# Attention thresholds made on the scalar engine instead of the vector engine

## The chip, the cores and the metric

The kernel runs on one core of a Trainium2 chip. Its time is device microseconds (us) of one execution, start to end. Five engines work at once, each through its own queue in order: TensorE (PE, matrix products; its weight loads are listed as PEld), VectorE (DVE), ScalarE (ACT), GpSimd (POOL) and SyncE (SP, which here issues DMA transfers). They wait for each other on semaphores.

## What is computed

Attention over 4 batches, 8 heads, 576 positions, 64 dimensions, in which only scores close to the row's maximum count; its output goes through a mixture of experts with a greedy assignment of tokens, and through a gated feed-forward layer. The change is in the attention alone, whose reference is:

```python
scores = scale * np.matmul(q, k.transpose(0, 1, 3, 2))
thresh = np.max(scores, axis=-1, keepdims=True) - tau
scores = np.where(scores >= thresh, scores, -1000000000.0)
scores = scores - np.max(scores, axis=-1, keepdims=True)
attn = np.exp(scores)
attn = attn / (np.sum(attn, axis=-1, keepdims=True) + 1e-09)
return np.matmul(attn, v).astype(np.float32)
```

## The kernel before

The attention is cut into 16 units; a unit is one head of two batches and has nine score tiles of 128 rows by 576 columns. A score tile goes through these steps:

- PE makes the scores in PSUM, `s` (L248).
- DVE takes the negated maximum of each row, `nm` (L259), one column of a buffer of two columns that two successive tiles share.
- ACT makes `e` = exp(s + nm) (L263).
- For every second tile DVE makes the thresholds `th` of both tiles of the pair at once, a 128x2 result (L267): minus `nm`, minus the non-negative part of tau (`taup`, made once).
- DVE masks: `p` = e where s >= th, else 0, with the row sum on the way (L281). Both masks of a pair need `th`; the mask of the even tile comes first.
- PE transposes `p` (L289). The transposed blocks `t` are split into two parts, `hi` and `lo`, on ACT (L319, L322, L327, L344), DVE (L346, L349) and POOL (L185, L335); PE multiplies with the values (L361, L365, L373), ACT copies out `ot` (L378), PE multiplies again (L389, L394), and ACT scales by `ri`, one over the row sum (L416), which DVE makes (L401, L402).

POOL meanwhile prepares the next units' inputs (L198, L202, L212, L220 and again L185). DVE also converts pieces of the later layers' weights in three steps (L583, L585, L587), and at the end of a group of eight heads it sums the router's logits (L436, L439, L441).

The order of the work on every engine is written out beforehand. Each step has a name and a time in a table, `TAB` (the last two units: `LAST`), for two units together, a period of 2 x 18.2795 us; all steps are sorted by time, and each engine gets its own in that order. The times in the table decide the order alone; at run time an engine waits only for its semaphores. The two score buffers are freed by the masks, so PE's next scores wait for them. Four pairs of `nm` and `th` are kept.

After the attention (about the first 355 us) come the routing of tokens and the experts' products, in an order that a planner makes from costs of its own.

Of the kernel before, what the change touches and what calls it, by code (L numbers as in the profile page):

```python
# [7 lines left out]
F32 = mybir.dt.float32  # L8
# [3 lines left out]
AF = mybir.ActivationFunctionType  # L12
OP = mybir.AluOpType
# [112 lines left out]
def attention(tc, raw, prep, qk, v, tau, wg, xd, lg, idf, filler, chosen):  # L126
    nc = tc.nc
    with (
# [10 lines left out]
        taur = cp.tile([128, 1], F32, name="taur")  # L139
# [2 lines left out]
        warm = cp.tile([128, 1], F32, name="warm")  # L142
        nid = cp.tile([128, 128], F32R, name="nid")
        c = cp.tile([128, 1], F32, name="c")
        taup = cp.tile([128, 1], F32, name="taup")

        def constants():
            nc.vector.memset(warm, 0.0)
            nc.scalar.activation(warm, warm, AF.Exp)
            nc.vector.tensor_scalar(nid, idf, -1.0, None, op0=OP.mult)  # L150
            for o in (0, 64):
                nc.vector.tensor_copy(r2[o : o + 64, :, 0:64], idf[o : o + 64, o : o + 64].unsqueeze(1).to_broadcast([64, 8, 64]))
            nc.vector.tensor_scalar(c, taur, 0.0, 0.125, op0=OP.is_ge, op1=OP.mult)
            nc.vector.tensor_scalar(taup, taur, 0.0, None, op0=OP.max)

        def load_wg():
            for o in (0, 64):
# [3 lines left out]
        ev = []  # L161
# [2 lines left out]
            ev.append((t, len(ev), fn, args))  # L164

        def on(u, name, fn, *args):
            ev.append((2 * P * (u // 2) + (LAST if u >= 14 else TAB)[name], len(ev), fn, args))

        def types(u):
            return (LAST_TYPES if u >= 14 else TYPES)[u % 2]  # L170
# [93 lines left out]

        def sthr(n):
            nm, th = nmth[n // 2]
            nc.vector.tensor_scalar(th, nm, -1.0, taup, op0=OP.mult, op1=OP.subtract)  # L267

        def smask(u, i, n):
            w = d[u]  # L270
# [172 lines left out]
        P = PERIOD  # L443
        V, A, G = nc.vector, nc.scalar, nc.gpsimd
        for u in range(16):
            t = P * u
            pu = u % 2
            at(-100 + u if u < 2 else t - 2 * P, "", load, u)
            if u == 0:
                for n, (lo, hi) in enumerate(((0, 128), (128, 512), (512, 896), (896, 1280))):  # L450
                    steps = split_q(u, lo, hi, A, V)
                    if n < 2:
                        at(-20 + 2 * n, "", run, steps)
                    else:
                        at(TAB["exp1"] + 0.01 * n, "", next, steps)
                        at(TAB["mask1"] + 0.01 * n, "", next, steps)
                for n, (lo, hi) in enumerate(((0, 288), (288, S), (S, KW))):
                    at(-20.5 + 0.5 * n if n < 2 else -17, "", run, split_k(u, lo, hi, A, V if n < 2 else G))
                at(-15, "", run, split_v(u, G))
            else:  # L460
                steps = split(u)
                for n in range(12):
                    on(u, f"pp{pu}.{n}", next, steps)
            for i in range(9):
                n = 9 * u + i
                on(u, f"mm{n%18}", scores, u, i)
                on(u, f"max{n%18}", smax, u, i, n)
                on(u, f"exp{n%18}", sexp, u, i)
                if n % 2:
                    on(u, f"thr{n%18}", sthr, n)  # L470
                on(u, f"mask{n%18}", smask, u, i, n)
            for i in range(11):
# [13 lines left out]
                if i in (4, 10):  # L486
# [3 lines left out]
                    on(u, f"xl{pu}.{w}", l_out, u, w)  # L490
        at(-60, "", load_wg)
        at(-101, "", constants)
        at(14 * P + 40.4, "", chosen, slice(0, 9))
        at(14 * P + LAST["xl1.0"] + 0.01, "", chosen, slice(9, 13))
# [1025 lines left out]
def program(tc, qk, v, tau, wg, w12, cst, csti, w3, out):  # L1520
    nc = tc.nc
    with tc.tile_pool(name="keep", bufs=1) as kp, tc.tile_pool(name="keep_dram", bufs=1, space=bass.MemoryType.DRAM) as dp:
        idf = kp.tile([128, 128], F32, name="idf")
        make_identity(nc, idf)
        lg = kp.tile([128, 18, 8], F32, name="lg")
        xd = dp.tile([2304, 512], F32, name="xd")
        wf = [dp.tile([128, 512], F32, name=f"wf{n}") for n in range(36)]
        words = w3.bitcast(I32)
        rt = Router(tc, lg, idf, kp, dp)
        pre = n_pieces()  # L1530
        with (
            tc.tile_pool(name="at_raw", bufs=2) as rp, tc.tile_pool(name="at_prep", bufs=2) as pp,
            tc.tile_pool(name="staging", bufs=2) as sp,
        ):
            weights = Narrow(
                nc, lambda s: sp.tile([128, 1024], I32, name="wd", bufs=4), lambda n: sp.tile([128, 512], F32, name="wn", bufs=3),
                words, nc.sync, lambda n, f: nc.sync.dma_start(wf[n], f), {n: n % 4 for n in range(pre)},
            )
            filler = fill(rt.prepare(cst, csti), weights, 4)
            attention(tc, rp, pp, qk, v, tau, wg, xd, lg, idf, filler, rt.begin)  # L1540
        experts(tc, rt, xd, idf, w12, words, wf, pre, out)
# [14 lines left out]
```

## Time and profile before

| | |
|---|---|
| Median of 3 runs | 1146.61 us (1145.21 to 1149.75) |
| Profiled execution | 1150.95 us, of which the span of the profile is 1149.2 us |
| Busy over the span | PE 93%, DVE 71%, ACT 45%, POOL 28% |

The span holds very different stages, so the shares of the whole tell little of the attention. In the profile's rows, an entry gives the start and length in us, the engine, the line of the kernel, the operation, out<-in with shapes, a count where equal neighbours are merged, and in brackets the idle time before it with what ended it. A row of stretches gives, for each engine, its busy time in the stretch.

### The profile page before, as it was taken

What the parts mean: (1) busy time and instruction counts of PE and PEld (TensorE: products, weight loads), DVE (VectorE), ACT (ScalarE), POOL (GpSimd) and SP (SyncE); (2) the same over time, 40 slices, a digit from 0 to 9 for tenths busy, and PEclk for the clock granted to TensorE, in tenths of its full rate; (3) what the DMA queues carried; (4) which work ended last, traced back from release to release, by engine and by line L of the source; (5) the groups of instructions that cost most, each with busy time, mean ns of one, the idle gap of its engine ahead of it and who ended that gap; (6) DMA issues with size and microseconds to landing.
All of it is one profiled execution on the core that took longest, in us unless ns stands there. A gap on an engine that the chain in (4) does not pass through costs nothing.

```text
span 1149.2 us, 21045 instructions
## 1 busy us (share of the span) xinstructions
PE 1068.4 (93%) x7884; PEld 990.7 (86%) x7885; DVE 819.8 (71%) x1987; ACT 517.6 (45%) x1104; POOL 323.9 (28%) x334
## 2 busy tenths in 40 slices
PE   4899999999997399999899999999999999999997
PEld 3787878787886268899899999999999899999996
DVE  7999999899998799886776975974974412512411
ACT  4788887688784224333214314313413412412411
POOL 5788887788861101000101010110100100100101
PEclk9999999899998599999899999999999999999999
DMA  7422422422303766537436446546444433533232
GB/s 275 147 85 82 157 84 84 155 85 81 102 1 108 265 222 222 201 130 192 130 98 193 147 132 156 164 119 168 150 129 135 148 111 111 167 111 117 74 113 88
DMA packets 52886, 156.18 MB, mean 136 GB/s; under 512 B 11568, under 2 KB 16560, under 8 KB 50864
## 3 DMA queue, kind: packets, MB, share of 16 engines
q1 hardware_dynamic: 49712, 145.40, 39.5%
q0 software_dynamic: 3072, 9.44, 2.7%
q8 instruction: 62, 1.02, 0.4%
q14 instruction: 40, 0.33, 0.1%
HBM read 135.38 MB, written 19.43 MB: 135 GB/s over the span
## 4 chain that ended last, share of the span: by engine, by line
PE 40%; issue 26%; DVE 25%; DMA 4%; ACT 2%; POOL 2%; SPq 0%; DVEq 0%; POOLq 0%; ACTq 0%
PE ps L1144 18%; PE acc L1154 11%; DVE nm L259 6%; DVE p L281 6%; PE s L248 4%; DVE th L267 3%; DVE lo L346 2%; PE t L289 2%; DMA wr<-in_w 1%; PE o L365 1%; DMA wf<-wf 1%; PE o L373 1%; DVE wf L1088 1%; POOL out L1386 1%; DMA wd<-in_w 1%
## 5 line engine op out<-in xcount | busy, mean ns | idle before, releaser
L1330 DVE TENSOR_TENSOR gt<-ps,sg 128x288 f32<-128x288 f32 x96 | 43.9, 457 | 164.5 <-PE ps L1144 132.9
L1386 POOL DMA_INDIRECT out<-orow,idx x24 | 24.8, 1032 | 408.4 <-ACT orow L1382 404.0
L1326 ACT ACTIVATE sg<-ps 128x288 f32<-128x288 f32 x96 | 39.5, 412 | 193.8 <-PE ps L1144 169.2
L1154 PE MATMUL acc<-gh,wo 128*128 128x288 f32 x768 | 124.6, 300 | 0.9 <-DVE wo L1052 0.9
L263 ACT ACTIVATE e<-s,nm 128x576 f32<-128x576 f32 x144 | 104.9, 741 | 37.6 <-DVE nm L259 35.3
L1052 DVE TENSOR_TENSOR w<-wr,w 128x512 fp32r<-128x512 f32 x112 | 75.6, 689 | 54.7 <-ACT w L1225 53.8
L1144 PE MATMUL ps<-yh,wgh 128*128 128x288 f32 x384 | 107.2, 301 | 6.8 <-ACT orow L1382 4.4
L248 PE MATMUL s<-kh,qs 128*128 128x288 f32 x320 | 80.3, 333 | 34.5 <-DVE p L281 23.6
L1334 ACT ACTIVATE gh<-gt 128x288 fp32r<-128x288 f32 x96 | 42.7, 444 | 149.9 <-DVE gt L1330 149.9
L1154 PEld LDWEIGHTS acc<-gh,wo 128*128 128x128 f32 x768 | 108.3, 189 | 1.2 <-DVE wo L1052 1.1
L259 DVE TENSOR_REDUCE nm<-s 128x1 f32<-128x576 f32 x144 | 104.1, 747 | 5.3 <-PE s L248 4.5
L1144 PE MATMUL ps<-yh,wvh 128*128 128x288 f32 x384 | 107.3, 301 | 0.0
L1169 POOL DMA_INDIRECT xr<-xd,idx x16 | 15.2, 951 | 323.8 <-issue 158.0
L1144 PE MATMUL ps<-yh,wvl 128*128 128x288 f32 x384 | 106.1, 298 | 0.0
L1144 PE MATMUL ps<-yh,wgl 128*128 128x288 f32 x384 | 105.8, 297 | 0.0
L1225 ACT ACTIVATE w<-wr 128x512 fp32r<-128x512 f32 x112 | 69.2, 629 | 75.8 <-PE acc L1154 31.9
L281 DVE SCALAR_TENSOR_TENSOR p<-s,th,e 128x576 f32<-128x576 f32 x128 | 100.1, 808 | 4.3 <-ACT tf L319 0.5
L248 PEld LDWEIGHTS s<-kh,qs 128*128 128x128 f32 x320 | 52.7, 198 | 55.5 <-issue 36.3
L289 PE MATMUL t<-idf,p 128*128 128x128 f32 x548 | 81.5, 282 | 0.9 <-ACT lo L344 0.7
L1144 PEld LDWEIGHTS ps<-yh,wgh 128*128 128x128 f32 x384 | 72.8, 189 | 8.7 <-ACT orow L1382 4.9
L763 DVE TENSOR_SCALAR_CACHE_REDUCE big<-kw,tw 128x1152 bf16<-128x1152 f32 x56 | 78.9, 1409 | 1.0
L289 PEld LDWEIGHTS t<-idf,p 128*128 128x128 f32 x548 | 66.0, 145 | 14.0 <-ACT tf L319 2.2
(233 smaller groups left out, 2794.8 us busy)
## 6 DMA issues: line engine op xcount, KB each, us to landing
wo<-wod SPq DMA_DIRECT2D x84, 512.0 KB, 3.6
wr<-in_w SPq DMA_DIRECT2D x64, 512.0 KB, 3.8
qkr<-in_qk SPq DMA_DIRECT2D x15, 1248.0 KB, 5.7
wd<-in_w SPq DMA_DIRECT2D x36, 512.0 KB, 5.1
wod<-wo SPq DMA_DIRECT2D x12, 512.0 KB, 3.3
vr<-in_v SPq DMA_DIRECT2D x16, 320.0 KB, 3.8
kw<-kx SPq DMA_DIRECT2D x64, 72.0 KB, 4.2
xd<-xl SPq DMA_DIRECT2D x8, 512.0 KB, 4.0
```

Of the source, the lines that this page charges most:

```text
L248: nc.tensor.matmul(s[:, h, 0:288], qs[:, qo : qo + 128], kt[:, ko + 288 * h : ko + 288 * h + 288], start=m == 0, stop=m == len(src) - 1,)
L259: nc.vector.tensor_reduce(d[u]["nm", i], d[u]["s", i][:, :, 0:288], op=OP.max, axis=AX.XY, negate=True)
L263: nc.scalar.activation(e, d[u]["s", i][:, :, 0:288], AF.Exp, bias=d[u]["nm", i])
L281: nc.vector.scalar_tensor_tensor(dst.rearrange("p (c n) -> p c n", c=2), w["s", i][:, :, 0:288], nmth[n // 2][1][:, n % 2 : n % 2 + 1], w[ ...
L289: nc.tensor.matmul(t[:m, 128 * j : 128 * j + 128], src, idf, is_transpose=True, start=j == 0, stop=j == len(srcs) - 1, skip_group_check=True,)
L763: v.tensor_scalar(self.big, self.kw[h], thr, None, op0=OP.is_ge, op1=OP.add, accum_out=cnt[:, h : h + 1])
L1052: V.tensor_sub(l, x, h.bitcast(F32))
L1144: nc.tensor.matmul(ps, w(q), x[:, q], start=n == 0, stop=n == 11)
L1154: nc.tensor.matmul(acc[m][:, :CAP], w[:, 128 * m : 128 * m + 128], x, start=first and i == 0, stop=last and i == 2)
L1225: A.activation(box[nm][:, 0], box["r"][:, i], AF.Copy)
L1330: V.tensor_tensor(box["gt"], box["v"][:, :CAP], box["sg"], op=OP.mult)
L1334: A.activation(box["h"][0], box["gt"], AF.Copy)
```

## The change

The thresholds are made by ACT: `th` = Identity(-1 x nm + ntau), where `ntau` is the negated non-negative part of tau. In the order of the work the step stands where it stood, or directly ahead of the odd tile's exponential (0.01 before it in the table) where that came earlier.

```diff
@@ -142,7 +142,7 @@
-        taup = cp.tile([128, 1], F32, name="taup")
+        ntau = cp.tile([128, 1], F32, name="ntau")
@@ -151,7 +151,7 @@
-            nc.vector.tensor_scalar(taup, taur, 0.0, None, op0=OP.max)
+            nc.vector.tensor_scalar(ntau, taur, 0.0, -1.0, op0=OP.max, op1=OP.mult)
@@ -164,7 +164,9 @@
         def on(u, name, fn, *args):
-            ev.append((2 * P * (u // 2) + (LAST if u >= 14 else TAB)[name], len(ev), fn, args))
+            tab = LAST if u >= 14 else TAB
+            t = min(tab[name], tab["exp" + name[3:]] - 0.01) if name[:3] == "thr" else tab[name]
+            ev.append((2 * P * (u // 2) + t, len(ev), fn, args))
@@ -264,7 +266,7 @@
         def sthr(n):
             nm, th = nmth[n // 2]
-            nc.vector.tensor_scalar(th, nm, -1.0, taup, op0=OP.mult, op1=OP.subtract)
+            nc.scalar.activation(th, nm, AF.Identity, bias=ntau, scale=-1.0)
```

## Rows read from the trace of the kernel before

**Rows 1.** The chain of work that ended last, 0 to 400 us, by line.

```profile
by line: DVE nm L259 16.5%; DVE p L281 16.4%; PE s L248 12.3%; DVE th L267 7.3%; DVE lo L346 5.6%; issue 4.9%; PE t L289 4.9%; PE o L365 3.4%; DMA wf<-wf 3.1%; PE o L373 3.0%; DVE pt L281 1.7%; PE o L361 1.6%; DVE hl L349 1.4%; PE o L389 1.
```

**Rows 2.** Busy time by stretch (two units; two at a group's end): PE, PEld, DVE, ACT, POOL, granted clock, DMA.

```profile
99.24:140.76 41.52, 39.74 (x277) 33.53 (x276) 40.70 (x86) 34.30 (x73) 35.14 (x34) 1.00 0.39 125
...
182.22:230.20 47.98, 43.54 (x277) 37.37 (x276) 42.59 (x89) 34.53 (x73) 35.24 (x34) 0.89 0.33 109
```

**Rows 3.** Line L267 as a group: whole kernel, one stretch of two units, shortest/median/longest.

```profile
L267 DVE TENSOR_SCALAR th<-nm,taup 128x2 f32<-128x2 f32 x72 | 47.1, 654 | 1.2
...
L267 DVE TENSOR_SCALAR th<-nm,taup 128x2 f32<-128x2 f32 x9 | 6.3, 699 | 0.1
...
L267 DVE TENSOR_SCALAR th<-nm,taup x72: 220/572/1548, 9.3 to 347.4; 128x2 f32<-128x2 f32 x72
```

**Rows 4.** DVE in order of time, the stretch from 99 to 142 us.

```profile
100.70 0.53 DVE L267 TENSOR_SCALAR th<-nm,taup 128x2 f32<-128x2 f32 x1
101.14 0.41 DVE L583 TENSOR_SCALAR wn<-wd 128x512 int32<-128x512 int32 x1
...
104.99 0.95 DVE L267 TENSOR_SCALAR th<-nm,taup 128x2 f32<-128x2 f32 x1
105.86 0.16 DVE L401 TENSOR_SCALAR ri<-sm 128x9 f32<-128x9 f32 x1
...
110.73 0.98 DVE L267 TENSOR_SCALAR th<-nm,taup 128x2 f32<-128x2 f32 x1
...
119.87 0.88 DVE L267 TENSOR_SCALAR th<-nm,taup 128x2 f32<-128x2 f32 x1
120.66 0.68 DVE L587 SCALAR_TENSOR_TENSOR wn<-wd,wn 128x512 int32<-128x512 int32 x1
...
124.78 0.23 DVE L267 TENSOR_SCALAR th<-nm,taup 128x2 f32<-128x2 f32 x1
125.11 0.82 DVE L281 SCALAR_TENSOR_TENSOR p<-s,th,e 128x576 f32<-128x576 f32 x1
...
128.64 1.16 DVE L267 TENSOR_SCALAR th<-nm,taup 128x2 f32<-128x2 f32 x1
```

**Rows 5.** POOL in order of time, the same stretch.

```profile
104.37 1.55 POOL L202 TENSOR_TENSOR qs<-qkr,qs 64x640 fp32r<-64x640 f32 x1
...
122.90 1.56 POOL L202 TENSOR_TENSOR qs<-qkr,qs 64x640 fp32r<-64x640 f32 x1
...
128.29 1.48 POOL L212 TENSOR_TENSOR kl<-qkr,kh 128x608 fp32r<-128x608 f32 x1
```

**Rows 6.** DVE and POOL around 198 us.

```profile
197.83 1.00 DVE L585 SCALAR_TENSOR_TENSOR wn<-wd,wn 128x512 int32<-128x512 int32 x1
...
197.56 0.72 POOL L185 TENSOR_SCALAR vh<-vr 128x640 fp32r<-128x640 f32 x1
```

**Rows 7.** ACT's table load, its smallest instruction, and 128x64 ones, as groups.

```profile
L416 ACT ACTIVATE xl<-o,ri 128x64 f32<-128x64 f32 x139 | 31.8, 329 | 0.6 <-PE o L389 0.6
...
L149 ACT ACT_TABLE_LOAD x1 | 1.3, 1283 | 0.7 <-PEq L1549 0.7
...
L149 ACT ACTIVATE warm<-warm 128x1 f32<-128x1 f32 x1 | 0.2, 203 | 0.0
```

**Rows 8.** ACT in order of time, around the odd tiles' exponentials.

```profile
119.27 1.40 ACT L263 ACTIVATE e<-s,nm 128x576 f32<-128x576 f32 x2 [0.52 <-DVE nm L259]
...
133.47 0.59 ACT L319 ACTIVATE tf<-t 128x512 f32<-128x512 f32 x1
...
138.16 0.38 ACT L378 ACTIVATE ot<-o 128x256 f32<-128x256 f32 x1 [0.33 <-PE o L373]
```

**Rows 9.** DVE and PE at 201 to 204 us, and the stretch 206 to 208 us.

```profile
201.22 1.55 DVE L267 TENSOR_SCALAR th<-nm,taup 128x2 f32<-128x2 f32 x1
...
203.85 0.50 PE L248 MATMUL s<-kh,qs 128*128 128x288 f32 x2 [1.88 <-DVE pt L281]
...
206.00:208.00 2.00, 2.00 (x16) 1.87 (x15) 1.97 (x4) 1.47 (x3) 1.84 (x2) 0.50 0.00 1
```

## The prediction

> **What bounds the kernel now.** I read first the chain of work that ended last, for the first 400 us, since the change touches nothing behind the attention. Half of it is DVE: row maxima, masks, splits, and 7.3% on the threshold line itself, which is 29 us of 400 [rows 1]. The reader is to see that a 128x2 instruction stands there beside 128x576 ones.
>
> Second, the busy times by stretch. Two units take 41.5 us, in which DVE is busy for 40.7; it idles 0.8. But PE is busy for 39.7, POOL for 35.1 and ACT for 34.3 [rows 2]. So DVE paces the attention, and PE is only 1.8 us behind it. That is the second thing to see: whatever DVE gives up beyond about 1.8 us in a stretch meets PE, unless part of PE's modelled busy time is itself waiting.
>
> Third, the threshold line as a group: 72 instructions, 47.1 us, mean 654 ns, but from 220 to 1548 ns for one and the same shape [rows 3]. Idle time ahead of them is 1.2 us in all. So the time is spent inside the instruction, and it is not work.
>
> Fourth, therefore, DVE and POOL side by side in order of time. The threshold that starts at 104.99 and takes 0.95 ends at 105.94; the POOL instruction that was running ends at 104.37 + 1.55 = 105.92. The one at 128.64 ends at 129.80, POOL's at 129.77. The one at 124.78 takes 0.23, and POOL's instruction had ended at 124.46 [rows 4, 5]. So this instruction waits for whatever POOL is running. The Trainium skill's page "SBUF — State Buffer", section "Who interferes with whom", states a cause: a tensor_scalar can take a port pair that DVE shares with GpSimd, which is held for a whole instruction, while ACT waits for nobody. The end times above agree with it.
>
> **The change part by part.** The constant `ntau` in place of `taup` is one instruction at the start either way: nothing.
>
> *Taken from DVE.* In a stretch of two units the nine thresholds take 6.3 us. At 0.22 each without a wait that is 2.0 of work and 4.3 of waiting; over the kernel 72 x 0.22 = 15.8 and 31.3 [rows 3]. That is the upper end: 47.1 us, if nothing takes their place.
>
> *What the waits pass on to.* After three of the nine, DVE's next instruction is one that may wait for POOL too: L583 at 101.14, `ri` at 105.86, L587 at 120.66 [rows 4]. The first two are of the same kind as the threshold, and ran at 0.41 and 0.16 because the threshold had waited ahead of them. L587 is of L585's kind; an L585 began at 197.83 beside a POOL instruction that ended at 198.28, and took 1.00, where the L587 above took 0.68 [rows 6]. So I let all three inherit the wait: of 0.53 + 0.95 + 0.88 I count as saved only the step itself, about 0.13 each after overlap with its neighbours, 0.4 together. The page named above has a rule that speaks against the change here: a DVE instruction with two SBUF inputs also contends with a GpSimd one that reads SBUF. By it L587 inherits in full; without it 0.75 us more a stretch would be saved.
>
> *What takes the threshold's place at the mask.* In the six others no such instruction follows. The even tile's mask now waits for ACT. Without a wait for POOL the old path was 0.03 us from maximum to threshold, and 0.33 from the threshold's start to the mask (124.78 to 125.11) [rows 4]: 0.36. The trace has no such instruction on ACT. Bounds: below, a 128x1 one, 0.203; above, one of 128x64 with a scale from memory, 0.329 [rows 7]. I take 0.25, since two columns are nearer to one than to 64. Where ACT is free, the odd exponential follows the odd maximum by about 0.1: the maximum ends as the threshold of 119.87 begins, and of the two exponentials from 119.27 to 120.67 the second began at about 119.97 [rows 4, 8]. The threshold now comes in its place: 0.1 + 0.25, and as much again as the first 0.1 for the signal back, so the mask begins 0.45 after the maximum, against 0.36 before. Other page, other price: "ScalarE: Activation LUTs", section "What ACT_TABLE_LOAD costs", gives about 280 ns with a pointer as bias, less 93 ns of overlap; by it the mask would begin at about 0.48.
>
> Now the six. Two have long waits and nothing else in the way: 0.98 at 110.73, where another split stands ahead of the mask and covers the ACT path (saves 0.9), and 1.16 at 128.64 (saves 0.85). Two have short ones, as the 0.23 at 124.78: they lose or gain 0.1, together nothing. In the last two ACT does something else ahead of the odd exponential. At 133.47 a 0.59 us copy is in ACT's queue ahead of the threshold, so the mask loses about 0.15. At 138.16 a copy that waits for PE stands between threshold and odd exponential [rows 8]; the odd mask then waits for that exponential, which comes 0.2 later than now, and what is gained at the even mask is not kept: zero, between -0.2 and +0.4.
>
> Sum for one stretch: 0.4 + 0.9 + 0.85 + 0.0 - 0.15 = 2.0 us. PE's idle time is 1.8 [rows 2]. ACT gains nine steps of 0.25, 2.2 us, and goes from 34.3 to 36.5 of some 40 us; it stays below the pace, but queue order makes a part of it felt. I take 1.5 us of the 2.0. Eight stretches: 12 us.
>
> *The clock.* One stretch is 6.5 us longer than the others, 47.98 against 41.5, with a mean granted clock of 0.89 [rows 2]. There DVE's threshold waited 1.55 us at 201.22, PE then idled 1.88 us for the mask, and at 206 to 208 us the clock stood at 0.50, its 1.2 GHz level [rows 9]. Without that wait PE's pause would be about 0.5 us. If no drop follows, some 4 us come back; since another drop in that stretch has another origin, and other pauses can appear elsewhere, I count half: 2 us.
>
> Behind the attention all order stays, and the work moves forward with its end. Total: 12 + 2 = 14 us. The profiled execution's 1150.95 us would be 1137; it stands 4.3 us above the median of the runs, so against 1146.61 the forecast is **1132.6 us**.
>
> **The rivals.**
>
> *A large gain.* POOL's instructions shift against DVE's, the inherited waits fall on POOL's pauses, and PE's busy time shrinks since part of it is waiting. For it: 31 us of waiting is twice what I count. Against it: PE at 39.7 of 41.5. With 3 us a stretch and the full 4 us of clock: 24 + 4 = 28, so 1119 us.
>
> *Nothing comes through.* The waits pass to L583, L587, `ri`, and at the other masks the ACT path replaces what is saved; PE takes the rest. For it: seven of the nine positions come out at about nothing in the sum above. Against it: the two long waits have no heir. Then 0.5 us a stretch, 4 us: 1142 to 1150 us.
>
> *ACT becomes the bound, and the kernel slower.* The place is the odd exponential: it now stands behind the threshold on ACT, and the odd mask behind it. ACT already waits on PE in front of such places [rows 8]. The point from which it decides: the threshold cost DVE 0.65 on average [rows 3], so the masks must come out more than that later by ACT. If every pair waits the 0.25 of the new ACT step and a further 0.6 of queue ahead of it, that is 0.2 more than now, 72 x 0.2 = 14 us: 1161. Against it: ACT has 7 us idle in a stretch [rows 2], and before the exponentials of 119.27 it waited 0.52 for DVE's maximum: there it is early, not late. The Trainium skill's page "ScalarE: Activation LUTs", section "Rules for kernel authors", would have additions and products on VectorE, which speaks for this rival as far as the work alone goes (0.25 against 0.22); the trace's waits speak against it.
>
> *A table switch at each threshold.* If Identity were not in the table that Exp uses, 144 loads would come in. The trace has no Identity; the copies between exponentials cause none. A load took 1.283 us [rows 7], so it would be 185 us on ACT, to about 1300 us. Hardly likely.
>
> **How the numbers follow.** My forecast, a gain of 8 to 22 us: 0.55. Large gain: 0.14. Nothing, within 0.5% (5.7 us, about what a measurement of this kernel can tell): 0.18. ACT as bound: 0.11. Table: 0.02. The gains of 6 to 8 us go with the forecast. So faster 0.69, same 0.18, slower 0.13. The range leaves out the far part of the large gain and the slower cases: 1117 to 1147 us; the forecast's own is 1124 to 1139.
>
> **What would show it.** No threshold on DVE; 72 on ACT at 0.2 to 0.3 us each. Stretches of two units at about 40 us instead of 41.5. `ri` (0.16 behind a threshold now), L583 (0.41) and L587 (0.68) longer: the inherited waits. On DVE, short idle times ahead of masks, ended by ACT. PE's idle time in a stretch below 1 us. A full-speed clock from 204 to 212 us would show the clock term. The prediction is wrong if masks wait for odd exponentials by more than 0.3 us on average, if POOL's waits find no heir, or if PE gets well below 39 us busy in a stretch.

## The result, and the profile after

The changed kernel takes 1128.08 us (median of 4 runs, 1127.01 to 1131.51), the kernel before 1148.03 (4 runs, the three of the table above and one more, 1145.21 to 1149.75). The ratio is 0.9837, 95% interval 0.982 to 0.9855: faster by 1.6%. The forecast was 1132.6 us, in a range of 1117 to 1147; the gain was forecast at 14 us and is 20.0. The profiled execution took 1127.83 us, its span 1126.0; it is 23 us shorter than the profiled one of before, whose 1150.95 us is longer than any of that kernel's four runs here.

The busy times of two stretches, one of the usual kind and the one at the end of a group of eight heads (columns as in [rows 2]):

```profile
89.71:129.08 39.37, 38.90 (x277) 33.41 (x276) 36.43 (x78) 35.20 (x83) 35.12 (x34) 1.00 0.40 133
...
168.43:209.47 41.04, 38.83 (x277) 33.51 (x276) 37.97 (x80) 35.40 (x83) 36.08 (x34) 1.00 0.39 127
```

Against [rows 2], the usual stretch went from 41.52 to 39.37 us. DVE, which idled 0.8 us, now idles 2.9. PE idles 0.5 instead of 1.8, and its busy time fell by 0.8 though it does the same 277 matmuls: part of "busy" was waiting. ACT's busy time rose by 0.9. The other stretch went from 47.98 to 41.04, with the clock at 1.00 throughout.

The threshold as a group on ACT, with those who waited for it:

```profile
L269 ACT ACTIVATE th<-nm,ntau x72: 282/295/327, 9.3 to 325.7; 128x2 f32<-128x2 f32 x72
...
  DVE p L283: 13.3, 34
  DVE pt L283: 2.0, 7
```

Here the reader sees what [rows 3] lacked: nearly the same time for every instance, 0.28 to 0.33 us. The last threshold starts at 325.7 instead of 347.4, so 21.7 of the 23 us between the two profiled executions lie in the attention. The price is in the fence's last two lines: 15.3 us in which a DVE mask waited for it.

The chain that ended last, 0 to 378 us, to set beside [rows 1]:

```profile
by line: PE s L250 21.5%; PE t L291 13.6%; PE o L367 6.8%; PE o L391 6.5%; DVE nm L261 6.2%; PE o L363 5.7%; PE o L375 5.5%; issue 4.1%; DVE p L283 3.8%; DMA wf<-wf 3.3%; DVE lo L348 2.1%; PE t L339 1.9%; DVE ri L403 1.7%; PE o L396 1.5%; D
```

Where half of it was DVE, most of it is now PE. Whether that means that PE alone sets the pace is a question for the experiments.

DVE's groups before (first fence) and after (second), 0 to 400 us, for the instructions that were to inherit the waits, and after the change the masks:

```profile
L585 DVE SCALAR_TENSOR_TENSOR wn<-wd,wn 128x512 int32<-128x512 int32 x13 | 10.4, 797 | 0.0
...
L587 DVE SCALAR_TENSOR_TENSOR wn<-wd,wn 128x512 int32<-128x512 int32 x13 | 9.4, 725 | 0.0
L583 DVE TENSOR_SCALAR wn<-wd 128x512 int32<-128x512 int32 x13 | 5.4, 417 | 0.0
L401 DVE TENSOR_SCALAR ri<-sm 128x9 f32<-128x9 f32 x16 | 5.4, 338 | 0.0
```

```profile
L283 DVE SCALAR_TENSOR_TENSOR p<-s,th,e 128x576 f32<-128x576 f32 x128 | 100.7, 810 | 15.5 <-ACT th L269 13.3 <-ACT e L265 2.1
...
L403 DVE TENSOR_SCALAR ri<-sm 128x9 f32<-128x9 f32 x16 | 11.3, 705 | 0.0
L587 DVE SCALAR_TENSOR_TENSOR wn<-wd,wn 128x512 int32<-128x512 int32 x13 | 10.4, 799 | 0.0
L589 DVE SCALAR_TENSOR_TENSOR wn<-wd,wn 128x512 int32<-128x512 int32 x13 | 9.5, 732 | 0.0
L585 DVE TENSOR_SCALAR wn<-wd 128x512 int32<-128x512 int32 x13 | 8.5, 655 | 0.0
```

All lines of the kernel behind the edit moved down by two. The two tensor_scalars inherited waits: `ri` went from 5.4 to 11.3 us, the first step of the weights from 5.4 to 8.5, together 9.0 of the 31.3 us of waiting. The groups of the scalar_tensor_tensors (before L585 and L587, now L587 and L589) stayed as they were. Of these only the third step, L587 before and L589 now, ever stood directly behind a threshold (7 times of 13), so it alone could inherit.

Single places in the stretch, DVE first, then POOL:

```profile
99.72 1.09 DVE L403 TENSOR_SCALAR ri<-sm 128x9 f32<-128x9 f32 x1
...
112.50 1.36 DVE L261 TENSOR_REDUCE nm<-s 128x1 f32<-128x576 f32 x2
113.77 0.68 DVE L589 SCALAR_TENSOR_TENSOR wn<-wd,wn 128x512 int32<-128x512 int32 x1
114.37 0.81 DVE L283 SCALAR_TENSOR_TENSOR p<-s,th,e 128x576 f32<-128x576 f32 x1
...
120.72 1.41 DVE L261 TENSOR_REDUCE nm<-s 128x1 f32<-128x576 f32 x2
122.50 0.82 DVE L283 SCALAR_TENSOR_TENSOR p<-s,th,e 128x576 f32<-128x576 f32 x1 [0.36 <-ACT th L269]
...
126.99 0.82 DVE L283 SCALAR_TENSOR_TENSOR p<-s,th,e 128x576 f32<-128x576 f32 x1 [0.68 <-ACT th L269]
```

```profile
99.22 1.56 POOL L204 TENSOR_TENSOR qs<-qkr,qs 64x640 fp32r<-64x640 f32 x1
...
113.17 0.72 POOL L187 TENSOR_SCALAR qs<-qkr 128x640 fp32r<-128x640 f32 x1
113.97 1.91 POOL L204 TENSOR_TENSOR qs<-qkr,qs 64x640 fp32r<-64x640 f32 x1
```

`ri` at 99.72 ends at 100.81, POOL's instruction at 100.78: the wait of [rows 4] has moved to the next in line. L589 at 113.77 did not wait visibly, but when it began, POOL's L187 had only 0.12 us left (to 113.89). POOL's next instruction, begun 0.2 us after L589, took 1.91 instead of 1.56. The Trainium skill's page "SBUF — State Buffer", section "Who interferes with whom", has it that whoever issues first holds the shared port; the trace agrees as far as that one pair goes. The same step in the other order, with POOL first, stands under thr_late below; there it does wait. Before, the mask of this pair came 2.79 us after the start of its maxima (118.47 to 121.26), now 1.87 (112.50 to 114.37):

```profile
118.47 1.36 DVE L259 TENSOR_REDUCE nm<-s 128x1 f32<-128x576 f32 x2
...
121.26 0.81 DVE L281 SCALAR_TENSOR_TENSOR p<-s,th,e 128x576 f32<-128x576 f32 x1
```

A mask with nothing between begins 0.37 us after the odd maximum (122.13 to 122.50); in the last pair of the stretch, where a copy stands ahead on ACT, it waits 0.68.

### The profile page after: what moved, and what is told of

Its sections match the earlier page's. It is cut to its first block, busy times and chain, and to the rows that moved or that the text cites. A ratio compares the mean times of both kernels' runs of the same rounds, so it can differ in the third digit from the quotient of the medians.

```text
span 1126.0 us, 21012 instructions
## 1 busy us (share of the span) xinstructions
PE 1055.1 (94%) x7885; PEld 983.5 (87%) x7885; DVE 787.3 (70%) x1915; ACT 525.4 (47%) x1176; POOL 324.2 (29%) x334
## 4 chain that ended last, share of the span: by engine, by line
PE 51%; issue 26%; DVE 14%; DMA 4%; ACT 2%; POOL 2%; SPq 0%; POOLq 0%; ACTq 0%; DVEq 0%
PE ps L1146 17%; PE acc L1156 11%; PE s L250 7%; PE t L291 5%; PE o L367 2%; PE o L391 2%; DVE nm L261 2%; PE o L363 2%; PE o L375 2%; DMA wr<-in_w 2%; DVE p L283 1%; DMA wf<-wf 1%; POOL out L1388 1%; DVE wf L1090 1%; DMA wd<-in_w 1%
## 5 line engine op out<-in xcount | busy, mean ns | idle before, releaser
L283 DVE SCALAR_TENSOR_TENSOR p<-s,th,e 128x576 f32<-128x576 f32 x128 | 100.7, 810 | 15.5 <-ACT th L269 13.3
L291 PE MATMUL t<-idf,p 128*128 128x128 f32 x548 | 78.4, 277 | 0.7 <-ACT lo L346 0.7
```

The lines of the kernel that those rows point to most:

```text
L283: nc.vector.scalar_tensor_tensor(dst.rearrange("p (c n) -> p c n", c=2), w["s", i][:, :, 0:288], nmth[n // 2][1][:, n % 2 : n % 2 + 1], w[ ...
L291: nc.tensor.matmul(t[:m, 128 * j : 128 * j + 128], src, idf, is_transpose=True, start=j == 0, stop=j == len(srcs) - 1, skip_group_check=True,)
```

## The experiments

Two theories of the gain were put to the test. **A**: the gain is DVE's wait for POOL. **B**: it is one instruction less on DVE, or an earlier threshold on ACT. After them come the clock, what sets the pace since the change (**PE alone**, or something shared), and the place of the threshold on ACT. Times in the headings are medians, the ratio is to the kernel before in the same session.

**dve_reduce** (1129.92 us, ratio 0.9839, 0.9812 to 0.9866): the threshold goes back to DVE, in another form. Tau lies beside the negated maximum in a tile, written once, and the sum of the two, negated, is the threshold. The main line is shown against the changed kernel; the tile's set-up is not shown.

```diff
-            nc.scalar.activation(th, nm, AF.Identity, bias=ntau, scale=-1.0)
+            nc.vector.tensor_reduce(th, nm, op=OP.add, axis=AX.X, negate=True)
```

> The threshold is again made by DVE, at its old place in the order, but by a sum over two neighbouring values (negated maximum and tau) instead of a tensor_scalar; nothing is left out. Theory A (the gain is the wait for POOL inside the old instruction, and PE paces since): the new instruction takes 0.15 to 0.25 us each time, with no spread that follows POOL, stretches of two units stay at 39.3 to 39.6 us, and the time is that of the changed kernel, 1125 to 1132 us. Theory B (the gain comes from having one instruction less on DVE, or from ACT making the threshold earlier): DVE has its 72 instructions back, stretches go back to 41 us or more, 1142 to 1149 us.

The threshold's group and a stretch of dve_reduce:

```profile
L272 DVE TENSOR_REDUCE th<-nmt x72: 143/157/175, 9.3 to 325.3; 128x2 f32<-128x4 f32 x72
```

```profile
90.53:129.58 39.05, 38.60 (x277) 33.40 (x276) 37.34 (x87) 33.90 (x74) 35.23 (x34) 1.00 0.40 133
```

An instruction on DVE at the old place, with next to no spread, gives the whole gain: theory A. ACT was not needed for it. B falls. That what the old form waits for is POOL is seen in the trace of before: of its 72 thresholds 55 took more than 0.3 us, and all 55 end 0.02 to 0.03 us after the end of a POOL instruction.

**spare_ts** (1145.02 us, ratio 0.9973, 0.9958 to 0.9989) and **spare_red** (1130.86 us, ratio 0.9855, 0.9829 to 0.988): the changed kernel with a second, unread threshold on DVE at the old place, once in the old form and once as a reduction (one line of each is shown).

```diff
+            nc.vector.tensor_scalar(du, nmth[n // 2][0], -1.0, ntau, op0=OP.mult, op1=OP.add)                  # spare_ts
+            nc.vector.tensor_reduce(du, nmth[n // 2][0].unsqueeze(2), op=OP.add, axis=AX.X, negate=True)       # spare_red
```

> The changed kernel, and DVE makes the old tensor_scalar as well, at its old place, into a buffer that nobody reads. Theory A: the waits for POOL come back (mean 0.6 to 0.7 us, 47 us in all), stretches of two units are at 41.3 us or more, 1143 to 1152 us. Theory B' (only DVE's own work counts, 72 x 0.22 = 16 us, and DVE idles 2.9 us of 39.35 in a stretch now, which takes up the 2.0): 1128 to 1132 us.

> The changed kernel, and DVE makes a 128x2 tensor_reduce of the same buffer as well, at the old place, into a buffer that nobody reads. As many DVE instructions as with the spare tensor_scalar. Theory A: it does not wait for POOL, takes about 0.15 us, and disappears in DVE's idle time while PE paces: 1126 to 1133 us. Theory B (the number of DVE instructions in that place): as slow as with the spare tensor_scalar, 1143 us or more.

The spare instruction as a group, and a stretch, in spare_ts and in spare_red:

```profile
L273 DVE TENSOR_SCALAR du<-nm,ntau x72: 223/653/1592, 9.3 to 342.2; 128x2 f32<-128x2 f32 x72
```

```profile
94.15:135.51 41.36, 39.89 (x277) 33.53 (x276) 40.51 (x87) 35.64 (x83) 35.12 (x34) 1.00 0.37 125
```

```profile
L273 DVE TENSOR_REDUCE du<-nm x72: 141/155/157, 9.2 to 325.8; 128x2 f32<-128x2 f32 x72
```

```profile
89.50:128.84 39.34, 38.91 (x277) 33.46 (x276) 37.12 (x86) 35.17 (x83) 35.22 (x34) 1.00 0.41 135
```

Both have 72 more DVE instructions of one shape at one place; nobody reads their result. The one that spreads from 223 to 1592 ns takes the stretch back to 41.36 us, the other leaves it at 39.34. That is theory A once more, and it shows too that it is the wait, not the work, that was worth 2 us a stretch. Theory B' falls with it.

**pause** (1131.3 us, ratio 0.9864, 0.9832 to 0.9896): the clock. Three more row maxima on DVE in the fifth stretch, one at pair 37, two at pair 40 (only the place is shown).

```diff
+                    if n // 2 in (37, 40):
+                        on(u, f"thr{n%18}", pause, u, i, 1 if n // 2 == 37 else 2)   # unread row maxima
```

> The changed kernel with three more row maxima (0.7 us each, results unread) on DVE in the fifth stretch alone: one ahead of the mask where the old threshold cost 0.6 us at 185, two where it cost 1.55 us at 201. Clock theory (a pause of PE of about 1.9 us ahead of the mask brought the clock down, and that was worth 4 to 5 us): the granted clock shows 0.5 for several us after at least one of the pauses, the fifth stretch goes from 41.05 to 45 us or more, the time is up by 4 to 7 us, to 1132 to 1135 us. Rival (that stretch only lost DVE's own time): the stretch grows by at most 2.2 us and the clock stays at 1.0, 1128 to 1130 us.

That stretch, PE's two pauses in it, and the windows behind the first:

```profile
170.04:214.02 43.98, 40.61 (x277) 34.82 (x276) 39.30 (x83) 35.66 (x83) 36.05 (x34) 0.96 0.36 119
```

```profile
179.06 0.50 PE L250 MATMUL s<-kh,qs 128*128 128x288 f32 x2 [1.83 <-DVE p L288]
195.98 0.50 PE L250 MATMUL s<-kh,qs 128*128 128x288 f32 x2 [1.54 <-DVE pt L288]
```

```profile
179.00:181.00 2.00, 1.94 (x10) 1.79 (x11) 1.92 (x4) 2.00 (x8) 1.92 (x2) 0.81 0.00 0
181.00:183.00 2.00, 2.00 (x10) 1.70 (x9) 1.82 (x5) 1.23 (x4) 0.29 (x1) 0.50 0.00 0
```

The changed kernel itself, at the same places, and the kernel before at the first of them (its second is in [rows 9]):

```profile
177.36 0.50 PE L250 MATMUL s<-kh,qs 128*128 128x288 f32 x2 [1.76 <-DVE p L283]
191.36 0.50 PE L250 MATMUL s<-kh,qs 128*128 128x288 f32 x2 [0.21 <-DVE pt L283]
```

```profile
186.76 0.50 PE L248 MATMUL s<-kh,qs 128*128 128x288 f32 x2 [1.81 <-DVE p L281]
```

```profile
188.00:190.00 2.00, 2.00 (x10) 1.71 (x9) 1.93 (x6) 1.15 (x2) 1.00 (x1) 0.50 0.00 0
190.00:192.00 2.00, 2.00 (x11) 1.31 (x10) 0.81 (x3) 1.55 (x3) 0.89 (x2) 0.65 0.03 8
```

After the first pause, of 1.83 us, the clock fell to its lower level; after the second, 1.54 us, it did not. The stretch grew by 2.9 us, between the two expectations: one drop instead of the two of before. The median is 3.2 us higher, but the intervals of the two ratios overlap, so the times alone decide nothing. At the first place the three kernels have almost the same pause, 1.81 us before, 1.76 in the changed kernel and 1.83 here, and a drop follows it in the first and the third only. So the length of this pause does not explain why the drop went, and at the second place a pause of 1.54 us did not bring the drop back. That pauses cause the drops was not shown; it stays open.

**less_pe** (1129.55 us, ratio 0.9859, 0.9836 to 0.9883): less work for PE alone (the edit stands at two places).

```diff
-                    for x in (hi, lo):
+                    for x in (hi, lo) if i in (0, 4, 8) else (hi,):
```

> The changed kernel without the products of the low parts of the masked scores with the values in six of nine blocks of a unit (12 matmuls of 0.23 us fewer in two units; this part of the result is left out). PE theory (since the change PE paces the attention): stretches of two units fall from 39.35 to between 37 and 38.5 us, the time by 8 to 16 us, to 1112 to 1120 us. Rival (the coupling of DVE and ACT still sets the pace, PE's busy time is filled by waiting): stretches stay above 39 us, 1125 to 1130 us.

**dve_reduce_ri** (1123.61 us, ratio 0.981, 0.9789 to 0.983): less waiting on DVE.

```diff
-            nc.vector.tensor_scalar(ri, d[u]["sm"], 1e-9, None, op0=OP.add)
-            nc.vector.reciprocal(ri, ri)
+            nc.vector.reciprocal(ri, d[u]["sm"])
```

> As dve_reduce, and the addition of 1e-9 to the row sums, a DVE tensor_scalar that waits for POOL, is dropped (a row sum is at least 1, where it changes nothing in single precision). DVE loses about 1.8 us a stretch of two units. PE theory: stretches stay at 38.6 to 39.1 us, 1124 to 1130 us. Rival (DVE still paces, so each wait for POOL that goes is a gain): stretches near 37.2 us, 1112 to 1118 us.

**less_both** (1122.5 us, ratio 0.9793, 0.9745 to 0.9841): both together.

> less_pe and dve_reduce_ri together: the products of the low parts left out in six of nine blocks (this part of the result is left out), the threshold by a DVE sum, no addition of 1e-9. Theory C (since the change PE's chain and the chain through DVE lie within 0.3 us of each other in a stretch, so that cutting either alone gains little): together they gain more than the sum of the parts (0.3 by less PE, 0.9 by less DVE): stretches at 36.5 to 37.8 us, 1110 to 1119 us. Rival D (a third limit, ACT or POOL at 35 us busy with its own waits, holds both): stretches at 38 us or more, 1120 to 1125 us.

**act_ri** (1126.16 us, ratio 0.9809, 0.9771 to 0.9846): the changed kernel without the addition of 1e-9, the threshold on ACT.

> The changed kernel without the addition of 1e-9 to the row sums (it changes nothing in single precision). Theory C (PE's chain, with the delays that ACT's thresholds put into it, holds at nearly 39 us): stretches at 38.8 to 39.3 us, 1124 to 1129 us. Rival (DVE's waits for POOL are still what counts): 1.8 us less a stretch, near 37.6 us, 1112 to 1117 us.

One stretch each of less_pe, dve_reduce_ri, less_both and act_ri, in this order, a fence for each:

```profile
89.55:128.61 39.06, 36.95 (x265) 31.36 (x264) 36.36 (x78) 35.29 (x83) 35.10 (x34) 1.00 0.40 134
```

```profile
90.10:128.54 38.44, 38.08 (x277) 33.48 (x276) 36.46 (x85) 33.76 (x74) 34.98 (x34) 1.00 0.41 135
```

```profile
88.57:126.49 37.92, 36.42 (x265) 31.40 (x264) 36.27 (x84) 33.79 (x73) 34.99 (x34) 1.00 0.41 137
```

```profile
90.10:129.01 38.91, 38.55 (x277) 33.51 (x276) 35.28 (x75) 35.14 (x83) 35.72 (x34) 1.00 0.40 133
```

The theory that PE alone paces fell. With 12 matmuls fewer, PE idled 2.1 us and the stretch lost only 0.3. The medians of less_pe and less_both hold something besides: from 330 to 340 us the clock of less_pe stood at 0.63 where the changed kernel's stood at 1.00, and in less_both's fifth stretch it stood at 0.96 on average. So the stretches are compared here, all at full clock. Taking `ri`'s wait from DVE gave 0.5 (39.37 to 38.91) with the threshold on ACT, and 0.6 (39.05 to 38.44) with it on DVE. Together, less PE and less DVE gave 1.45 against 0.31 + 0.93 for the two alone: a little more than the sum, but 37.92 lies between what theory C and its rival had foreseen, and the median, 1122.5, lies where the rival had it. No engine is full there (PE 36.4, DVE 36.3, POOL 35.0, ACT 33.8 of 37.9). From 90 to 128.1 us of less_both the chain that ended last runs through three of them in turn:

```profile
by line: PE s L253 19.3%; DVE nmt L264 12.5%; DVE p L286 12.3%; PE t L294 12.1%; PE o L378 9.1%; DVE lo L351 6.8%; PE o L394 6.7%; PE o L370 5.0%; issue 4.2%; ACT hi L327 2.9%; PE o L399 2.1%; PE t L342 1.8%; PE o L366 1.7%; ACT tf L324 1.6
```

What is shown is that the pace is shared by chains through PE and through DVE; which wait would go next stays open. dve_reduce_ri and act_ri, which compute the same result, each lie 22.4 us below the kernel before of their session, where the changed kernel was 20.0 below that of its own; the intervals overlap, so only the stretches show the further gain.

**thr_late** (1156.59 us, ratio 1.0101, 1.0084 to 1.0118), **spare_act** (1131.79 us, ratio 0.988, 0.9864 to 0.9897) and **thr_early** (1130.45 us, ratio 0.9844, 0.9808 to 0.988): ACT's side. The threshold behind the odd exponential; twice; further ahead (one line of each is shown).

```diff
+                t = min(tab["exp" + name[3:]] + 0.005, tab[f"mask{int(name[3:]) - 1}"] - 0.005)     # thr_late
+            nc.scalar.activation(du, nm, AF.Identity, bias=ntau, scale=-1.0)                        # spare_act
+            t = min(tab[name], tab["max" + name[3:]] + 0.6) if name[:3] == "thr" else tab[name]     # thr_early
```

> The changed kernel with ACT's threshold behind the odd tile's exponential, not ahead of it, in eight of nine pairs. The even mask then comes about 0.45 to 0.6 us later after the maximum. Theory (the place matters: the masks' waits for ACT go from 1.9 to 5 us or more in a stretch of two units, more than the 2.9 us that DVE idles now): stretches at 40 to 41 us, 1133 to 1143 us. Rival (PE's pace covers it): 1126 to 1131 us.

> The changed kernel with each of ACT's threshold instructions made twice, the second into a buffer that nobody reads: ACT gets 9 x 0.2 = 1.8 us more in a stretch of two units, as much as the change itself added. PE theory (ACT's new instructions cost nothing but their delay to the masks): stretches at 39.3 to 39.8 us, 1127 to 1133 us. Rival (ACT is so near to the pace that its new instructions ate part of the gain): 0.6 to 1.8 us more in a stretch, 1133 to 1143 us.

> The changed kernel with ACT's threshold put 0.6 behind the odd maximum's place in the table, ahead of other copies that stood before it (the copy ahead of the last pair's threshold among them). Theory (the place decides by the masks' waits; the last pair's 0.68 us goes to about 0.3, the others stay): 0 to 0.4 us less in a stretch, 1123 to 1130 us. Rival (ACT then waits for the odd maximum in front of copies that PE needs, and PE is late): 0.3 us or more added to a stretch, 1131 to 1140 us.

The masks' group in thr_late, a stretch of it, and the third step of the weights (L589 in the changed kernel) with the POOL instruction that was running:

```profile
L286 DVE SCALAR_TENSOR_TENSOR p<-s,th,e 128x576 f32<-128x576 f32 x128 | 100.6, 814 | 47.9 <-ACT th L272 47.9
```

```profile
96.71:139.89 43.18, 40.29 (x277) 33.66 (x276) 36.05 (x78) 35.67 (x81) 35.21 (x35) 1.00 0.36 121
```

```profile
122.33 1.52 DVE L592 SCALAR_TENSOR_TENSOR wn<-wd,wn 128x512 int32<-128x512 int32 x1
```

```profile
121.75 1.55 POOL L207 TENSOR_TENSOR qs<-qkr,qs 64x640 fp32r<-64x640 f32 x1
```

A stretch of spare_act, then one of thr_early, and in thr_early the mask that waited 0.68 us in the changed kernel:

```profile
91.14:130.89 39.75, 39.22 (x277) 33.49 (x276) 36.88 (x78) 36.71 (x92) 35.08 (x34) 1.00 0.39 131
```

```profile
89.97:129.39 39.42, 38.94 (x277) 33.41 (x276) 36.55 (x78) 35.32 (x83) 35.16 (x34) 1.00 0.39 132
```

```profile
126.92 0.82 DVE L283 SCALAR_TENSOR_TENSOR p<-s,th,e 128x576 f32<-128x576 f32 x1 [0.36 <-ACT th L269]
```

Behind the odd exponential, the same instruction makes the kernel slower than before: the masks wait 47.9 us for it where they waited 13.3, and a stretch takes 43.2 us. I had expected 40 to 41 us, and a kernel still faster than before; the direction was right, the size not. The weights' step adds to it: it began with 0.97 us of POOL's instruction left and took 1.52 us instead of 0.68. Twice the ACT instructions add 1.5 us to ACT's busy time in a stretch and 0.4 to the stretch: a quarter of ACT's new work is felt, within the first of the two expectations. Further ahead, the wait of 0.68 us became 0.36, as expected, and yet the stretch did not get shorter (39.42 against 39.37): neither expectation for the stretch came.

## Why the prediction was right

*The whole.* The gain was forecast at 14 us and is 20.0 between the medians here (18.5 from the median that the prediction started from). The stretches were counted with 12 us; eight times the 2.15 of a usual one is 17.2, so most of the miss is there. The range, 30 us wide, holds the result easily; what speaks for the prediction is the mechanism.

*The bound and the wait.* Right: DVE paced, and the time inside the 128x2 instruction was waiting for POOL. The end times of [rows 4, 5] had only suggested it; all 55 long thresholds of the trace end that way, and dve_reduce and the two spare forms show what it was worth.

*The sum for a stretch.* 2.0 us were summed and 1.5 taken; it was 2.15 (41.52 to 39.37). The term that was off is the three heirs: `ri` and L583 inherited as said (9.0 us in all), L587 did not. At its place 0.92 us were gained where 0.13 was counted. The step "So I let all three inherit the wait" failed there, and not because this kind of instruction does not wait: in thr_late the same step waited in full (1.52 us). It took for granted that POOL would stand beside DVE where it stood before. But DVE had come forward by one POOL instruction (the second `ri` of the stretch, at 117.58, waited for POOL's L198 before; now, at 111.62, it waits for the instruction ahead of that, L222), and L589 now met the last 0.12 us of one instead of the middle. That was luck of the order in time, which the prediction had named only in its rival of a large gain. For a stretch it is the 0.75 us that the prediction gave as the price of this doubt, which makes the sum 2.75. Of that, 0.6 did not come through; the 0.5 that I took off for PE and ACT was near that, though ACT's busy time rose by 0.9 us and not by 2.2.

*The ACT path.* Sized at 0.25 us for the instruction and 0.45 from maximum to mask; it was 0.295 and 0.37. At the pairs with nothing in between it therefore cost what the old path without a wait had cost (0.36 [rows 4]). The two places where ACT does something else first behaved as described: a mask that waits 0.68 us where a copy stands ahead of the threshold, and where one stands behind it, an odd mask that waits for its exponential (2.1 us over the kernel).

*PE as the next bound.* Half right. PE's idle time fell below 1 us as foreseen, but the remark that PE is "only 1.8 us behind" took modelled busy time for need, unless, as it said itself, part of that was waiting: 0.8 us of it went away by itself, and less_pe shows that PE's work alone does not hold the stretch.

*The clock.* Counted with 2 us at half weight. In the profiled executions the fifth stretch fell by 6.9 us, 4.8 more than a usual one, and both drops of before are gone, though the prediction had reckoned with one of them only. From the windows an estimate puts the first drop at 1.7 us (188 to 192 us) and the second at 3.4 (204 to 212), if time is lost as the clock falls short of 1. The medians probably hold less: the profiled execution of before had a mean clock of 0.969, 27 later runs of that kernel 0.969 to 0.977 with a median of 0.973, and the changed kernel's four runs 0.971 to 0.977. The cause stays open. At the second place the pause of 1.88 us became 0.21 and the drop went, as described; but at the first the drop went while the pause stayed at 1.76, and in pause 1.54 us at the second place brought none.

*The rivals.* The large gain came in part: POOL did shift against DVE at one heir, PE's busy time did shrink, and the clock stayed up; but a stretch gave 2.15 us and not 3, since the other chains were near, as said against it. ACT as the bound was a real danger, as thr_late shows, which is 10.6 us or 1% slower than before. Its kind was named rightly (ACT's queue order at the odd exponential), but there the masks wait for a threshold behind the exponential, not for an exponential behind the threshold. The order in the change, directly ahead of that exponential or earlier, is what avoided it. No table loads appeared.

## What to carry to other kernels

When a tiny instruction has a mean of several times its minimum and no idle time ahead of it, lay the other engines beside it in time before counting it as work: here its ends fell on POOL's, and changing its form on the same engine was worth as much as moving it. Then look who is next in line, since the wait can pass to the next instruction that waits for the same engine (`ri`, L583); whether it does depends on where that engine stands by then, and the change itself moves that. And when a small step that others wait for goes to an in-order queue, its place in that queue can decide the sign: behind the odd exponential instead of ahead of it turned 1.6% faster into 1% slower.

## What was not expected of the hardware

A DVE tensor_reduce of 128x2 to 128x2 took 0.141 to 0.157 us in all 72 instances of spare_red, with POOL busy for 35 of the 39 us of a stretch, where a tensor_scalar of the same shape in spare_ts took 0.223 to 1.592. The scalar_tensor_tensors of the weights waited by a plain rule. In the traces of all the kernels here, 132 of them began when a POOL instruction had 0.15 us or more left; 119 ended 0.53 to 0.55 us after that instruction's end (the 1.00 us at 197.83 [rows 6] and the 1.52 of thr_late are two of them), and in the other 13 it was the POOL instruction that took longer, such as 1.40 us instead of 0.72. So what a wait costs depends on where in POOL's instruction DVE arrives, and the 0.12 us left to L589 cost it nothing. And PE's busy time in a stretch of the same matmuls moved with the pace, from 39.74 us before to 38.08 in dve_reduce_ri.
